# Who transposes K, in which units, and in what order x and q0 are formed: six edits to the first third of a sliding-window attention kernel

## The chip, the cores and the metric

The kernel runs on one core of one Trainium2 chip. The metric is the device time of one execution in microseconds (us); lower is better. A time quoted for a kernel is the median of its runs, usually four: one with a profile and three timed rounds. Positions inside a kernel are microseconds from the start of the span of its one profiled execution, which is some 2 us shorter than the device time. Ratios are always against the kernel before in the same rounds on the same chip (medians 185.15 to 186.0 us), so compare kernels of different rounds by their ratios.

The engines are PE (matmuls and transposes through PE), PEld (PE's weight loads), DVE (vector), ACT (the exponentials), POOL (here used for small moves), and SP, which issues nearly all DMAs. PSUM is the memory that PE writes to in this kernel and that DVE and ACT copy out of.

## The reference

Eight sequences of 32 queries attend to the last 2,048 keys of a cache. There are 32 query heads and 4 K/V heads, so that 8 query heads share one K. Everything is bf16; the head size is 128.

```python
B, Sq, D = 8, 32, 1024
Hq, Hkv, Sk, Dh = 32, 4, 8192, 128
W = min(4096, max(256, Sk // 4))                  # 2048
q = transpose((x @ wq).reshape(B, Sq, Hq, Dh))
k = repeat(k_cache[:, :, Sk - W:, :], 8 heads); v = the same of v_cache
p = softmax((q @ k^T) * Dh ** -0.5)
out = transpose(p @ v).reshape(B, Sq, Hq * Dh) @ wo
```

## The kernel before

The work is cut into 32 units, one for each pair of K/V head and sequence. A unit's K is 2,048 x 128 and has 256 query columns. A unit has four slots, so that unit u is slots 4u to 4u+3. A slot is 4 score matmuls (`s_ps`), one exponential on ACT, and the 8 `o_ps` matmuls of the slot two earlier. Into slots PE also takes pieces of other work: transposes of a later K, the projections q1 to q3 of the later heads, and the output projection. I write S(n) for the start of slot n's score matmuls.

The score matmul needs K transposed. Three routes do it, chosen by unit:

- `PE_T`: K arrives as it is, PE transposes it in 16 pieces into PSUM, DVE copies it out.
- `V_T`: K arrives as it is, DVE turns its 32 x 32 blocks in four instructions (`kb`), then POOL puts the blocks in place in up to 16 moves (`kTv`).
- otherwise: two transposing DMAs, each of half of K (256 KB).

```python
Q_CUT = 6
N_WARM = (8, 0, 0)
PE_T = (0, 1, 2, 3, 4)
# unit: (load with unit, slots of the 4 DVE block transposes, first and end slot of the moves, moves on POOL of 16)
V_T = {5: (2, (5, 6, 8, 10), 10, 17, 12),
       **{u: (u - 4, range(4*u - 16, 4*u - 12), 4*u - 13, 4*u - 4, 16) for u in (8, 11, 14, 17, 20, 23, 26, 29)}}
Q_SLOTS = {1: (17, 31), 2: (38, 54), 3: (69, 83)}       # slots in which q1, q2, q3 are formed

def kv_pieces(self, ui):
    def blocks(i):                                         # DVE
        ...
        nc.vector.transpose(out=st["kb"][:, sl, :], in_=self.k_raw[ui][:, sl, :])
    def move(k, d):                                        # POOL, or DVE beyond the unit's share
        ...
        if d >= V_T[ui][4] // 4:
            nc.vector.tensor_copy(out=out, in_=in_)
        else:
            nc.gpsimd.tensor_scalar(out=out, in0=in_, scalar1=1.0, scalar2=1.0, op0=ALU.mult, op1=ALU.mult)
...
# the start: x in two tiles of 128 rows, on two queues
nc.sync.dma_start(out=x_sb[:, 0, :], in_=xf[0:P, :])
nc.scalar.dma_start(out=x_sb[:, 1, :], in_=xf[P:2 * P, :])
wq0 = self.load_wq(0, 0, (1, 1, 1, 1)) + self.load_wq(0, 1, (2, 1, 1))    # q0's weights, in 7 pieces
...
def x_turn(half, pl, tag):                 # both row tiles of one half of the columns
    ps = pl.tile([P, H, self.NT, P], BF16, name="xT_ps", tag=tag)
    for c in range(H):
        for t in range(self.NT):
            nc.tensor.transpose(ps[:, c, t, :], x_sb[:, t, half*H + c:self.D:self.DC], self.ident[:, :])
    for i, copy in ((0, nc.vector.tensor_copy), (1, nc.scalar.copy)):
        ...
x_turn(0, self.ps_m, "m")
x_turn(1, self.ps_s, "s_ps")
...
for c in range(self.DC):                   # q0: 8 heads; from c = 6 on only the first 128 rows
    for h in range(self.rep):
        q_mm(c, h, 0, P if c >= Q_CUT else self.NQ)
    ...
...                                        # the cut rest of q0 is done in slots 0 and 1
```

`N_WARM` counts the matmuls of no use that PE does before x has come.

POOL takes the moves in program order, and so does DVE its block transposes and copies; there are two buffers each for `kb` and `kTv`.

Of the kernel before, what the change touches and what calls it, by code (L numbers as in the profile page):

```python
# [18 lines left out]
Q_CUT = 6  # L19
N_WARM = (8, 0, 0)  # L20
# [3 lines left out]
PE_T = (0, 1, 2, 3, 4)  # L24

V_T = {5: (2, (5, 6, 8, 10), 10, 17, 12),
       **{u: (u - 4, range(4 * u - 16, 4 * u - 12), 4 * u - 13, 4 * u - 4, 16) for u in (8, 11, 14, 17, 20, 23, 26, 29)}}
W_AT = (3, 3, 4, 4, 8, 8, 9, 9, 11, 12, 13, 13, 14, 15, 16, 16, 18, 19, 19, 20, 22, 22, 23, 24, 25, 26, 28, 28)

Q_SLOTS = {1: (17, 31), 2: (38, 54), 3: (69, 83)}  # L30
# [74 lines left out]
class Fast:  # L105
# [101 lines left out]
    def load_unit(self, ui):  # L207

        if ui < len(self.units):
            if ui not in V_T:  # L210
                self.load_k(ui, None if ui in PE_T else 0)
            self.load_v(ui, self.nc.sync)
            if ui not in V_T and ui not in PE_T:
                self.load_k(ui, 1)
        for u, at in V_T.items():
            if at[0] == ui:
                self.load_k(u)
        for p, at in zip(self.weights, W_AT):
            if at == ui:
                p()  # L220
# [46 lines left out]
    def q_pieces(self, g):  # L267
        nc, P, DC = self.nc, self.P, self.DC
        st = {}

        def piece(hl, i):
            if i == 0:
                st["ps"] = self.ps_m.tile([P, 512], FP32, name="q_ps", tag="m")
            for c in range(i * DC // 2, (i + 1) * DC // 2):
                nc.tensor.matmul(st["ps"][:, 0:self.NQ], lhsT=self.wq_t[g, i][:, c % (DC // 2), hl * P:(hl + 1) * P],  # L275
                                 rhs=self.xT[:, c, :], start=(c == 0), stop=(c == DC - 1))
            if i == 1:
                nc.vector.tensor_copy(out=self.q_view(g)[:, :, hl, :],  # L278
                                      in_=st["ps"][:, 0:self.NQ].rearrange("p (b s) -> p b s", b=self.B))
        return [lambda h=h, i=i: piece(h, i) for h in range(self.rep) for i in range(2)]  # L280
# [31 lines left out]
    def start(self):  # L312
# [8 lines left out]
        nc.scalar.dma_start(out=x_sb[:, 1, :], in_=xf[P:2 * P, :])  # L321
# [25 lines left out]
        warm_up(N_WARM[0])  # L347


        def x_turn(half, pl, tag):  # L350
            ps = pl.tile([P, H, self.NT, P], BF16, name="xT_ps", tag=tag)
            for c in range(H):
                for t in range(self.NT):
                    nc.tensor.transpose(ps[:, c, t, :], x_sb[:, t, half * H + c:self.D:self.DC], self.ident[:, :])  # L354
            for i, copy in ((0, nc.vector.tensor_copy), (1, nc.scalar.copy)):
                c0 = half * H + i * H // 2
                copy(out=self.xT[:, c0:c0 + H // 2, :], in_=ps[:, i * H // 2:(i + 1) * H // 2, :, :].rearrange("p c t s -> p c (t s)"))

        x_turn(0, self.ps_m, "m")
        x_turn(1, self.ps_s, "s_ps")  # L360
        qs = [pl.tile([P, 2, self.NQ], FP32, name="q0_ps", tag=tag)
              for pl, tag in ((self.ps_o, "o_ps"), (self.ps_o, "o_ps"), (self.ps_m, "m"), (self.ps_m, "m"))]
# [11 lines left out]
        def q_mm(c, h, n0, n1):  # L374
            nc.tensor.matmul(qs[h // 2][:, h % 2, n0:n1], lhsT=self.wq_t[0, c // H][:, c % H, h * P:(h + 1) * P],  # L375
                             rhs=self.xT[:, c, n0:n1], start=(c == 0 and h % 2 == 0), stop=(c == self.DC - 1),
                             skip_group_check=True)

        for c in range(self.DC):
            for h in range(self.rep):  # L380
                q_mm(c, h, 0, P if c >= Q_CUT else self.NQ)
            if c == 0:
                warm_up(N_WARM[2])
                warm_sb = self.c1.tile([P, 8], BF16, name="warm_sb")
                nc.vector.tensor_copy(out=warm_sb[:, :], in_=warm[:, 0:8])
            if c == self.DC - 3:
                tp = self.ps_s.tile([P, KT, P], BF16, name="kf_ps", tag="s_ps")
                k_turn(0)
                k_copy(0)
        k_turn(1)  # L390

        def q_copy(eng, k, b0, b1):
            src = qs[k][:, :, :].rearrange("p h (b s) -> p b h s", b=self.B)[:, b0:b1, :, :]
            dst = self.q_view(0)[:, b0:b1, k * 2:(k + 1) * 2, :]
            (nc.vector.tensor_copy if eng == "v" else nc.scalar.copy)(out=dst, in_=src)
        for k, eng in ((0, "a"), (1, "v"), (2, "a"), (3, "v")):
            q_copy(eng, k, 0, 1)
        k_copy(1)
        self.va_copy(0)

        def q_rest(k):
            for h in (2 * k, 2 * k + 1):
                for c in range(Q_CUT, self.DC):
                    q_mm(c, h, P, self.NQ)
            q_copy("v", k, 1, self.B)
        self.q_rest = [lambda k=k: q_rest(k) for k in (0, 2, 3, 1)]
# [19 lines left out]
    def side_plan(self):  # L426
# [4 lines left out]
        def spread(pieces, s0, s1):  # L431
            for k, p in enumerate(pieces):
                plan[s0 + (s1 - s0) * k // len(pieces)].append(p)
        for g, w in Q_SLOTS.items():
# [10 lines left out]
    def run(self):  # L445
# [3 lines left out]
        for i, p in enumerate(self.q_rest):  # L449
            plan[i // 2].append(p)  # L450
# [205 lines left out]
```

## Time and profile before

The kernel took 185.55 us as given (185.06 to 186.25).

| what | before |
|---|---|
| span of the profile | 183.3 us |
| PE busy | 178.7 us, 98% |
| POOL busy | 94.7 us, 52% |
| first score matmul, S(0) | 12.92 us |
| S(31), S(32), S(48) | 51.12, 52.01, 70.73 us |
| last score matmuls, S(127) | 172.23 us |

The first fence has lines of the profile page: busy time of each engine with its share of the span and its instruction count; the shares of the chain that ended last, by engine; and two groups of instructions (line, engine, operation, output<-input, shapes, count | busy us, mean ns | idle us ahead of them and what ended most of it); and the transposing DMAs (count, median us from issue to landing).

```profile
PE 178.7 (98%) x2041; PEld 153.6 (84%) x2057; DVE 114.8 (63%) x266; ACT 131.6 (72%) x133; POOL 94.7 (52%) x150
...
PE 96%; DMA 2%; issue 1%; DVE 0%
...
L261 POOL TENSOR_SCALAR kTv<-kb 32x512 bf16<-32x512 bf16 x140 | 93.7, 670 | 63.8 <-PE s_ps L467 37.3
...
L236 PE MATMUL tp<-ident,k_raw 128*128 128x128 bf16 x64 | 5.9, 219 | 0.0
...
kT<-in_k_cache_dram SPq DMA_TRANSPOSE x36, 6.5
```

PE is the limit, and the chain says that it is so nearly everywhere. POOL looks half idle. The timeline of POOL shows what that average hides. Its columns are start in us, length in us, engine, line, operation, count, and in brackets the idle time before and what ended it.

```profile
27.03 8.77 POOL L261 TENSOR_SCALAR kTv<-kb 32x512 bf16<-32x512 bf16 x12 [25.46 <-PE s_ps L467]
38.44 11.77 POOL L261 TENSOR_SCALAR kTv<-kb 32x512 bf16<-32x512 bf16 x16 [2.64 <-PE s_ps L467]
53.18 11.65 POOL L261 TENSOR_SCALAR kTv<-kb 32x512 bf16<-32x512 bf16 x16 [2.97 <-DVE kb L251]
66.85 11.65 POOL L261 TENSOR_SCALAR kTv<-kb 32x512 bf16<-32x512 bf16 x16 [2.02 <-DVE kb L251]
```

These are the K of units 5, 8, 11 and 14, or K5, K8, K11 and K14 for short. The 16 moves of a K last 11.65 to 11.77 us, and POOL has two to three idle microseconds between them. K8 is ready at 50.21 and needed at 52.01; K11 is ready at 64.83 and needed at 65.42. So POOL just keeps up, with turned units that lie three apart.

The last fence is the timeline of PE, same columns: the start, then the score matmuls that open units 8, 9 and 12 (slots 32, 36 and 48).

```profile
4.50 1.33 PE L354 MATMUL xT_ps<-ident,x_sb 128*128 128x128 bf16 x16
5.84 5.40 PE L375 MATMUL q_ps<-xT,wq_sb 128*128 128x256 bf16 x48
12.92 0.60 PE L467 MATMUL s_ps<-QT,kT 128*128 128x256 bf16 x4
...
52.01 0.60 PE L467 MATMUL s_ps<-QT,kTv 128*128 128x256 bf16 x4
55.63 0.60 PE L467 MATMUL s_ps<-QT,kT 128*128 128x256 bf16 x4
70.73 0.60 PE L467 MATMUL s_ps<-QT,kT 128*128 128x256 bf16 x4
```

No line of PE carries a bracket: PE waits for nobody in all this stretch. Anything that makes it wait is paid in full.

### The profile page before, as it was taken

Reading aid. Unit: us, or ns where it says so; the run is one execution under the profiler, and the core shown is the slowest. Engines: PE = TensorE matmul, PEld = TensorE weight load, DVE = VectorE, ACT = ScalarE, POOL = GpSimd, SP = SyncE. Lnnn points to the kernel's source line nnn. Section 1 sums busy time; section 2 is a strip of 40 time slices with the busy share of each in tenths; the row PEclk is TensorE's granted clock in tenths of the full one; section 3 lists DMA queues with packets and bytes.
Section 4 is the critical chain, followed back from the end, with each engine's and each line's share of the span. In section 5 each row is a group of like instructions: output and inputs, shape, how many; then the busy total and the mean of one; then the engine's idle time right before and its main releaser. Section 6 shows DMA issues by size and latency. Waiting matters only on the chain.

```text
span 183.3 us, 5041 instructions
## 1 busy us (share of the span) xinstructions
PE 178.7 (98%) x2041; PEld 153.6 (84%) x2057; DVE 114.8 (63%) x266; ACT 131.6 (72%) x133; POOL 94.7 (52%) x150
## 2 busy tenths in 40 slices
PE   7999999999999999999999999999999999999993
PEld 2899999999999999987878999987787888888843
DVE  0238899975584774685567558647755865365363
ACT  2218999777799877777786687787877888888800
POOL 2000019759839959929945980896299279600000
DMA  6999999999999999999999999989999999960003
GB/s 173 392 405 407 397 402 367 186 249 397 258 307 303 384 240 325 401 246 249 378 380 227 374 389 224 245 327 386 242 371 345 216 272 286 229 185 1 0 32 93
DMA packets 52954, 51.73 MB, mean 282 GB/s; under 512 B 39744, under 2 KB 40256, under 8 KB 52928
## 3 DMA queue, kind: packets, MB, share of 16 engines
q1 hardware_dynamic: 52352, 50.90, 98.3%
q10 hardware_dynamic: 576, 0.49, 0.8%
q8 instruction: 16, 0.26, 0.6%
q14 instruction: 10, 0.08, 0.1%
HBM read 41.42 MB, written 0.52 MB: 229 GB/s over the span
## 4 chain that ended last, share of the span: by engine, by line
PE 96%; DMA 2%; issue 1%; DVE 0%
PE o_ps L478 32%; PE s_ps L467 31%; PE op_ps L295 14%; PE q_ps L275 11%; PE q_ps L375 4%; DMA x_sb<-in_x_dram 2%; PE tp L236 2%; PE xT_ps L354 1%; PE kf_ps L368 1%; DVE o_t L305 0%; PE cnt_ps L532 0%
## 5 line engine op out<-in xcount | busy, mean ns | idle before, releaser
L469 ACT ACTIVATE pT<-s_ps 128x1024 bf16<-128x1024 f32 x128 | 128.8, 1025 | 32.4 <-PE s_ps L467 31.4
L261 POOL TENSOR_SCALAR kTv<-kb 32x512 bf16<-32x512 bf16 x140 | 93.7, 670 | 63.8 <-PE s_ps L467 37.3
L478 PE MATMUL o_ps<-va,pT 128*128 128x129 bf16 x1024 | 78.8, 220 | 0.1
L478 PEld LDWEIGHTS <-pT 128*128 128x128 bf16 x1024 | 68.5, 98 | 3.1
L467 PE MATMUL s_ps<-QT,kT 128*128 128x256 bf16 x368 | 55.2, 273 | 0.2
L467 PEld LDWEIGHTS <-kT 128*128 128x128 bf16 x368 | 34.8, 98 | 10.3
L295 PE MATMUL op_ps<-wo_sb,OT 128*128 128x512 bf16 (+2 forms) x128 | 32.7, 352 | 0.6
L275 PE MATMUL q_ps<-xT,wq_sb 128*128 128x256 bf16 x192 | 28.1, 273 | 0.0
L409 DVE COPY va<-v_sb 128x2048 bf16<-128x2048 bf16 x32 | 25.3, 789 | 0.1
L251 DVE STREAM_TRANSPOSE kb<-k_raw 128x512 bf16<-128x512 bf16 x36 | 23.8, 685 | 0.0
L415 DVE RECIPROCAL RL_all<-o_ps 128x2 f32<-128x2 f32 x32 | 5.2, 164 | 27.5 <-PE o_ps L478 27.5
L467 PE MATMUL s_ps<-QT,kTv 128*128 128x256 bf16 x144 | 21.6, 272 | 0.0
L420 DVE TENSOR_SCALAR o_sb<-o_ps,RL_all 128x128 bf16<-128x128 f32 x64 | 19.5, 346 | 1.1
L467 PEld LDWEIGHTS <-kTv 128*128 128x128 bf16 x144 | 13.9, 98 | 5.1
L278 DVE CAST QT<-q_ps 128x256 bf16<-128x256 f32 x24 | 9.8, 406 | 13.4 <-PE q_ps L275 13.4
L275 PEld LDWEIGHTS <-wq_sb 128*128 128x128 bf16 x192 | 17.0, 98 | 1.2
L422 DVE STREAM_TRANSPOSE OT<-o_sb 128x256 bf16<-128x256 bf16 x32 | 14.3, 445 | 1.1
L295 PEld LDWEIGHTS <-OT 128*128 128x128 bf16 x144 | 11.4, 98 | 2.3 <-DVE OT L422 0.2
L302 DVE TENSOR_TENSOR oacc<-op_ps,oacc 128x512 f32<-128x512 f32 x8 | 5.5, 682 | 7.4 <-PE op_ps L295 7.4
L375 PE MATMUL q_ps<-xT,wq_sb 128*128 128x256 bf16 (+1 forms) x80 | 7.7, 251 | 0.0
L375 PEld LDWEIGHTS <-wq_sb 128*128 128x128 bf16 x80 | 6.7, 98 | 0.7
L236 PE MATMUL tp<-ident,k_raw 128*128 128x128 bf16 x64 | 5.9, 219 | 0.0
(30 smaller groups left out, 36.6 us busy)
## 6 DMA issues: line engine op xcount, KB each, us to landing
v_sb<-in_v_cache_dram SPq DMA_DIRECT2D x30, 512.0 KB, 7.0
wo_sb<-in_wo_dram SPq DMA_DIRECT2D x16, 512.0 KB, 6.5
wq_sb<-in_wq_dram SPq DMA_DIRECT2D x13, 512.0 KB, 7.3
k_raw<-in_k_cache_dram SPq DMA_DIRECT2D x13, 512.0 KB, 5.9
wq_sb<-in_wq_dram SPq DMA_DIRECT2D x6, 256.0 KB, 4.6
v_sb<-in_v_cache_dram SPq DMA_DIRECT2D x4, 256.0 KB, 4.8
kT<-in_k_cache_dram SPq DMA_TRANSPOSE x36, 6.5
k_raw<-in_k_cache_dram SPq DMA_DIRECT2D x2, 256.0 KB, 5.8
```

The lines of the kernel that those rows point to most:

```text
L251: nc.vector.transpose(out=st["kb"][:, sl, :], in_=self.k_raw[ui][:, sl, :])
L261: nc.gpsimd.tensor_scalar(out=out, in0=in_, scalar1=1.0, scalar2=1.0, op0=ALU.mult, op1=ALU.mult)
L275: nc.tensor.matmul(st["ps"][:, 0:self.NQ], lhsT=self.wq_t[g, i][:, c % (DC // 2), hl * P:(hl + 1) * P], rhs=self.xT[:, c, :], start=(c == ...
L278: nc.vector.tensor_copy(out=self.q_view(g)[:, :, hl, :], in_=st["ps"][:, 0:self.NQ].rearrange("p (b s) -> p b s", b=self.B))
L295: nc.tensor.matmul(ps[:, 0:w], lhsT=self.OT[:, gq, c, t * P:(t + 1) * P], rhs=self.wo_t[gq][:, c, n0:n0 + w], start=(k == 0), stop=(k == 7))
L375: nc.tensor.matmul(qs[h // 2][:, h % 2, n0:n1], lhsT=self.wq_t[0, c // H][:, c % H, h * P:(h + 1) * P], rhs=self.xT[:, c, n0:n1], start=(c ...
L409: self.nc.vector.tensor_copy(out=self.va[ui % 3][:, :, 0:self.Dh], in_=self.v_sb[ui][:, :, :])
L420: nc.vector.tensor_scalar(out=o_sb[:, qt, :, :], in0=o_ps[:, qt, 0:Dh].rearrange("p (i c) -> p c i", c=4), scalar1=rl[:, ui * QT_N + qt:ui ...
L422: nc.vector.transpose(out=self.OT[:, g * QT_N:(g + 1) * QT_N, :, b * self.Sq:(b + 1) * self.Sq], in_=o_sb[:, :, :, :])
L467: nc.tensor.matmul(s_ps[:, jj, :], lhsT=self.kT[ui][:, c * CJ + jj, :], rhs=q_u, start=True, stop=True)
L469: nc.scalar.activation(out=pT[:, :, :], in_=s_ps[:, :, :], func=ACT.Exp, bias=0.0, scale=self.scale)
L478: nc.tensor.matmul(o_ps[:, qt, 0:self.VW], lhsT=pT[:, jj, qt * P:(qt + 1) * P], rhs=va[:, j, 0:self.VW], start=(j == 0 and qt == 0), stop= ...
```

## The change

Six edits, meant to relieve PE or to let it start earlier:

1. K3 and K4 go from PE to transposing DMAs. That is 32 PE transposes less.
2. In exchange for DMA room, the V route turns units 8, 10, 12, 15, 17 and so on (not 8, 11, 14, 17): one K more, and closer together. Block transposes and moves are issued one slot later, those of unit 8 three slots later (the last block transpose in slot 22, not 19).
3. q0: the second row half of heads 4 to 7 leaves the start and is done in slots 0, 1, 8 and 10 (`q_late`).
4. q1 is formed from slot 14 on (in unit 3), not from slot 17, and its pieces are ordered so that the second half of its weights is needed later.
5. x is transposed by row tiles, the first tile without waiting for the second, and both tiles are loaded by SP's queue.
6. Where weights and the raw K of a V unit are loaded at the same unit, the weights now go first.

```diff
-Q_CUT = 6
-N_WARM = (8, 0, 0)
+N_WARM = 7
-PE_T = (0, 1, 2, 3, 4)
+PE_T = (0, 1, 2)
 V_T = {5: (2, (5, 6, 8, 10), 10, 17, 12),
-       **{u: (u - 4, range(4 * u - 16, 4 * u - 12), 4 * u - 13, 4 * u - 4, 16) for u in (8, 11, 14, 17, 20, 23, 26, 29)}}
+       8: (4, range(19, 23), 22, 30, 16),
+       **{u: (u - 4, range(4 * u - 15, 4 * u - 11), 4 * u - 12, 4 * u - 4, 16) for u in (10, 12, 15, 17, 20, 23, 26, 29)}}
-Q_SLOTS = {1: (17, 31), 2: (38, 54), 3: (69, 83)}
+Q_LATE = {0: (0, 2), 1: (8, 12)}
+Q_SLOTS = {1: (14, 31), 2: (38, 54), 3: (69, 83)}
 ... load_unit: the pieces of the weights ahead of the raw K of the V units
 ... q_pieces: two heads share a PSUM tile; for q1 four heads' first weight half comes before their second
+    def q_late(self, h0): ...      # rows 128 to 255 of two heads of q0, one PSUM tile, one DVE copy
-        nc.scalar.dma_start(out=x_sb[:, 1, :], in_=xf[P:2 * P, :])
+        nc.sync.dma_start(out=x_sb[:, 1, :], in_=xf[P:2 * P, :])
-        def x_turn(half, pl, tag): ...
+        def x_turn(t):
+            ps = self.ps_s.tile([P, 2, self.DC, P], BF16, name="xT_ps", tag="s_ps")
             for i, copy in ((0, nc.vector.tensor_copy), (1, nc.scalar.copy)):
+                for c in range(H):
+                    nc.tensor.transpose(ps[:, i, c, :], x_sb[:, t, i * H + c:self.D:self.DC], self.ident[:, :])
+                copy(out=self.xT[:, i * H:(i + 1) * H, t * P:(t + 1) * P], in_=ps[:, i, 0:H, :])
 ... the copies of q0 by row halves
```

More of the change, by code (lines that the diff above doesn't have):

```diff
@@ L214, in load_unit @@
                 self.load_k(ui, 1)
+        for p, at in zip(self.weights, W_AT):
+            if at == ui:
+                p()
         for u, at in V_T.items():
@@ L217, in load_unit @@
                 self.load_k(u)
-        for p, at in zip(self.weights, W_AT):
-            if at == ui:
-                p()
     def k_pieces(self, ui):
@@ L271, in piece @@
         def piece(hl, i):
+            k = hl // 2
+            if i == 0 and hl % 2 == 0:
+                st[k] = self.ps_m.tile([P, 2, self.NQ], FP32, name="q_ps", tag="m")
+            for c in range(i * DC // 2, (i + 1) * DC // 2):
+                nc.tensor.matmul(st[k][:, hl % 2, :], lhsT=self.wq_t[g, i][:, c % (DC // 2), hl * P:(hl + 1) * P],
+                                 rhs=self.xT[:, c, :], start=(c == 0 and hl % 2 == 0), stop=(c == DC - 1), skip_group_check=True)
+            if i == 1 and hl % 2 == 1:
+                nc.vector.tensor_copy(out=self.q_view(g)[:, :, 2 * k:2 * k + 2, :].rearrange("p b h s -> p h b s"),
+                                      in_=st[k][:, :, :].rearrange("p h (b s) -> p h b s", b=self.B))
@@ L272, in piece, with q_late @@
+        n = 4 if g == 1 else 2
+        return [lambda h=h, i=i: piece(h, i) for h0 in range(0, self.rep, n) for i in range(2) for h in range(h0, h0 + n)]
+    def q_late(self, h0):
+        nc, P, DC, B = self.nc, self.P, self.DC, self.B
+        st = {}
+        def piece(i):
             if i == 0:
-                st["ps"] = self.ps_m.tile([P, 512], FP32, name="q_ps", tag="m")
-            for c in range(i * DC // 2, (i + 1) * DC // 2):
-                nc.tensor.matmul(st["ps"][:, 0:self.NQ], lhsT=self.wq_t[g, i][:, c % (DC // 2), hl * P:(hl + 1) * P],
-                                 rhs=self.xT[:, c, :], start=(c == 0), stop=(c == DC - 1))
+                st["ps"] = self.ps_m.tile([P, 2, P], FP32, name="ql_ps", tag="m")
+            for c in range(DC):
+                nc.tensor.matmul(st["ps"][:, i, :], lhsT=self.wq_t[0, c // (DC // 2)][:, c % (DC // 2), (h0 + i) * P:(h0 + i + 1) * P],
+                                 rhs=self.xT[:, c, P:self.NQ], start=(c == 0 and i == 0), stop=(c == DC - 1), skip_group_check=True)
@@ L277, in piece @@
             if i == 1:
-                nc.vector.tensor_copy(out=self.q_view(g)[:, :, hl, :],
-                                      in_=st["ps"][:, 0:self.NQ].rearrange("p (b s) -> p b s", b=self.B))
-        return [lambda h=h, i=i: piece(h, i) for h in range(self.rep) for i in range(2)]
+                nc.vector.tensor_copy(out=self.q_view(0)[:, B // 2:, h0:h0 + 2, :].rearrange("p b h s -> p h b s"),
+                                      in_=st["ps"][:, :, :].rearrange("p h (b s) -> p h b s", b=B // 2))
@@ L282, in o_pieces @@
+        return [lambda i=i: piece(i) for i in range(2)]
     def o_pieces(self, g, t, cuts=(512, 512), st=None):
@@ L346, in warm_up @@
                 nc.tensor.matmul(warm[:, :], lhsT=one(1.0, [P, P], BF16), rhs=one(1.0, [P, 512], BF16), start=True, stop=True)
-        warm_up(N_WARM[0])
-        def x_turn(half, pl, tag):
-            ps = pl.tile([P, H, self.NT, P], BF16, name="xT_ps", tag=tag)
-            for c in range(H):
-                for t in range(self.NT):
-                    nc.tensor.transpose(ps[:, c, t, :], x_sb[:, t, half * H + c:self.D:self.DC], self.ident[:, :])
-            for i, copy in ((0, nc.vector.tensor_copy), (1, nc.scalar.copy)):
-                c0 = half * H + i * H // 2
-                copy(out=self.xT[:, c0:c0 + H // 2, :], in_=ps[:, i * H // 2:(i + 1) * H // 2, :, :].rearrange("p c t s -> p c (t s)"))
-        x_turn(0, self.ps_m, "m")
-        x_turn(1, self.ps_s, "s_ps")
-        qs = [pl.tile([P, 2, self.NQ], FP32, name="q0_ps", tag=tag)
-              for pl, tag in ((self.ps_o, "o_ps"), (self.ps_o, "o_ps"), (self.ps_m, "m"), (self.ps_m, "m"))]
+        warm_up(N_WARM)
+        warm_sb = self.c1.tile([P, 8], BF16, name="warm_sb")
+        nc.vector.tensor_copy(out=warm_sb[:, :], in_=warm[:, 0:8])
+        def x_turn(t):
+            ps = self.ps_s.tile([P, 2, self.DC, P], BF16, name="xT_ps", tag="s_ps")
+            for i, copy in ((0, nc.vector.tensor_copy), (1, nc.scalar.copy)):
+                for c in range(H):
+                    nc.tensor.transpose(ps[:, i, c, :], x_sb[:, t, i * H + c:self.D:self.DC], self.ident[:, :])
+                copy(out=self.xT[:, i * H:(i + 1) * H, t * P:(t + 1) * P], in_=ps[:, i, 0:H, :])
+        x_turn(0)
+        x_turn(1)
+        qs = [self.ps_o.tile([P, 2, self.NQ], FP32, name="q0_ps", tag="o_ps") for _ in range(2)]
+        qs.append(self.ps_m.tile([P, 4, P], FP32, name="q0_ps", tag="m"))
         KT = self.KT
@@ L372, in k_copy, with q_mm, q_copy @@
             nc.vector.tensor_copy(out=self.kT[0][:, sl, :], in_=tp[:, sl, :])
-        def q_mm(c, h, n0, n1):
-            nc.tensor.matmul(qs[h // 2][:, h % 2, n0:n1], lhsT=self.wq_t[0, c // H][:, c % H, h * P:(h + 1) * P],
-                             rhs=self.xT[:, c, n0:n1], start=(c == 0 and h % 2 == 0), stop=(c == self.DC - 1),
+        def q_mm(c, h):
+            ps, n = (qs[h // 2][:, h % 2, :], self.NQ) if h < 4 else (qs[2][:, h - 4, :], P)
+            nc.tensor.matmul(ps, lhsT=self.wq_t[0, c // H][:, c % H, h * P:(h + 1) * P],
+                             rhs=self.xT[:, c, 0:n], start=(c == 0 and h in (0, 2, 4)), stop=(c == self.DC - 1),
                              skip_group_check=True)
+        def q_copy(copy, h0, h1, b0, b1):
+            ps = qs[h0 // 2] if h0 < 4 else qs[2]
+            copy(out=self.q_view(0)[:, b0:b1, h0:h1, :].rearrange("p b h s -> p h b s"),
+                 in_=ps[:, :, b0 * self.Sq:b1 * self.Sq].rearrange("p h (b s) -> p h b s", s=self.Sq))
         for c in range(self.DC):
-            for h in range(self.rep):
-                q_mm(c, h, 0, P if c >= Q_CUT else self.NQ)
-            if c == 0:
-                warm_up(N_WARM[2])
-                warm_sb = self.c1.tile([P, 8], BF16, name="warm_sb")
-                nc.vector.tensor_copy(out=warm_sb[:, :], in_=warm[:, 0:8])
-            if c == self.DC - 3:
+            if c == self.DC - 2:
                 tp = self.ps_s.tile([P, KT, P], BF16, name="kf_ps", tag="s_ps")
@@ L389, in start @@
                 k_copy(0)
+            for h in range(self.rep):
+                q_mm(c, h)
         k_turn(1)
-        def q_copy(eng, k, b0, b1):
-            src = qs[k][:, :, :].rearrange("p h (b s) -> p b h s", b=self.B)[:, b0:b1, :, :]
-            dst = self.q_view(0)[:, b0:b1, k * 2:(k + 1) * 2, :]
-            (nc.vector.tensor_copy if eng == "v" else nc.scalar.copy)(out=dst, in_=src)
-        for k, eng in ((0, "a"), (1, "v"), (2, "a"), (3, "v")):
-            q_copy(eng, k, 0, 1)
+        q_copy(nc.scalar.copy, 0, 2, 0, 1)
+        q_copy(nc.vector.tensor_copy, 2, 4, 0, 1)
+        q_copy(nc.scalar.copy, 4, 8, 0, 1)
         k_copy(1)
         self.va_copy(0)
-        def q_rest(k):
-            for h in (2 * k, 2 * k + 1):
-                for c in range(Q_CUT, self.DC):
-                    q_mm(c, h, P, self.NQ)
-            q_copy("v", k, 1, self.B)
-        self.q_rest = [lambda k=k: q_rest(k) for k in (0, 2, 3, 1)]
+        q_copy(nc.vector.tensor_copy, 0, 2, 1, self.B)
+        q_copy(nc.vector.tensor_copy, 2, 4, 1, self.B)
+        q_copy(nc.vector.tensor_copy, 4, 8, 1, self.B // 2)
     def va_copy(self, ui):
@@ L433, in spread @@
                 plan[s0 + (s1 - s0) * k // len(pieces)].append(p)
+        for k, w in Q_LATE.items():
+            spread(self.q_late(4 + 2 * k), *w)
         for g, w in Q_SLOTS.items():
@@ L448, in run @@
         plan = self.side_plan()
-        for i, p in enumerate(self.q_rest):
-            plan[i // 2].append(p)
         pv_queue = []
```

## The prediction

> **What bounds it now.** PE. The page has PE busy 98% of 183.3 us; the chain of waits is 96% PE, and between 4.5 us (x lands) and about 172 us PE never waits. In the timeline a slot (4 score matmuls + 8 o_ps matmuls) takes 0.89 us bare, 1.11 with 4 K transposes, 1.33 with 4 q matmuls. ACT (1025 ns an exponential) is hidden except in bare slots (0.92). POOL looks idle half the time (52%), but by unit it is tight: the 16 moves of one V-turned K take 11.65 us on the timeline (12 moves of K5: 8.77), and end 0.3 us (K5), 1.8 (K8), 0.6 (K11), 0.7 (K29) before PE's first score of that unit.
>
> **What goes, costed from the trace.**
> - 32 PE transposes of K3, K4: 0.22 us per 4, so -1.8 us of PE.
> - x: tile 0's transposes no longer wait for tile 1; first q0 matmul about 0.4 us earlier.
> - q0: the same columns (4 heads x 128 rows moved out of the start), PE total unchanged; the start loses 0.9 us that returns in slots 0 to 10. But wq's third piece landed at 8.65 us, so about 0.5 us of the earlier start is spent waiting. First score at about 12.4 us (12.92 before).
> - Without new waits: -1.4 us, everywhere.
>
> **What it adds.**
> - DMA: K3 and K4 become transposing DMAs in the backlogged first 35 us. There a plain 512 KB landing costs 1.28 us (about 410 GB/s); a transposed half of K (256 KB) about 1.0 to 1.2. The Trainium skill, DMA: Bandwidth & Descriptors, Latency and other measured facts, gives 261 GB/s for a transposing DMA; the trace agrees roughly (210 to 260). K4's second half should land at 30 to 31.5 us, against a need at about 30.2; q1's second weight half at 33 to 34, against 33.8. I expect 0 to 2 us of PE waits here, 0.7 likely.
> - POOL, the large one. V now turns 8, 10, 12, 15 instead of 8, 11, 14. Spaced three units apart, 12 slots of 1.33 (16 us) covered 11.65. Two apart, 8 slots give 7 to 10.6 us. POOL cannot start K8 before its fourth block transpose, now issued in slot 22 (before: 19) behind q1's copy: about 2 us after slot 22's scores. Then K8, K10, K12 are 48 moves back to back, 35 us (the first four of K10 even stand before K8's last two). PE's own work from slot 22 to slot 48 (unit 12) is about 31 us. So PE must lose about 6 us, in three waits: before unit 8 about 2 to 2.5, before unit 10 about 2, before unit 12 about 1 to 1.5. Slot 48 starts near 76 us (70.7 before).
> - Later V units start one slot later than before; slack shrinks, K29 may cost 0.3 us.
> - DVE: about neutral (4 copies of 0.65 less, 4 block transposes of 0.69 more).
>
> **On the critical path:** PE's saving counts fully, but only until slot 22; POOL's queue then decides. From unit 12 on PE is dense again, as before, so nothing is won back.
>
> **Predicted:** 191.2 us, range 189.0 to 193.0. Faster 0.01, same 0.17, slower 0.82.
>
> **Signs.** Right: PE idle before s_ps of kTv tiles of units 8, 10, 12, about 6 us released by POOL kTv; POOL unbroken from about 40 to 76 us; kTv moves 156 at about 670 ns; transposes of K 32 on that line instead of 64; DMA-transposes 38. Slot 32 to 48 longer than 20 us.
>
> **Wrong if** POOL's moves run faster with less DVE traffic; if DMA waits for K3 or K4 are far larger (then slot 22 slips, more than 193); if slot 22's block transpose comes earlier than I place it (then 189).

## The result, and the profile after

The changed kernel took 193.75 us (192.66 to 194.5) against 185.31 us: slower by a ratio of 1.0445, 95% interval 1.0374 to 1.0515. A ratio is the mean time of one kernel's runs over that of the other's of the same rounds, so it is not quite the ratio of the medians quoted. The direction was as predicted, the size was not: 193.75 lies 0.75 us above the range of 189.0 to 193.0.

Lines of the changed kernel's page. The new one, PEclk, is the clock granted to PE in 40 equal slices of the span, in tenths; the kernel before has no such line.

```profile
PE 180.8 (94%) x2024; PEld 154.4 (81%) x2040; DVE 112.8 (59%) x254; ACT 131.6 (69%) x133; POOL 103.6 (54%) x166
...
PEclk9999999999996999999999999999999999999998
...
PE 81%; POOL 12%; DVE 2%; issue 2%; ACT 1%; ACTq 0%
...
L262 POOL TENSOR_SCALAR kTv<-kb 32x512 bf16<-32x512 bf16 x156 | 102.7, 658 | 63.3 <-DVE kb L252 38.5
...
kT<-in_k_cache_dram SPq DMA_TRANSPOSE x38, 7.1
```

POOL has come into the chain with 12%, and PE's share of the span fell to 94%. Next, the waits of PE in the changed kernel (who waited, for what: total us, how often, the longest).

```profile
PE s_ps L479 <- POOL kTv L262: 4.4, 3, 3.8
PE xT_ps L374 <- DVE xT L375: 1.0, 2, 0.5
```

POOL's timeline after. The 48 moves of K8, K10 and K12 are now a single line: unbroken from 43.61 to 77.97 us.

```profile
28.57 8.71 POOL L262 TENSOR_SCALAR kTv<-kb 32x512 bf16<-32x512 bf16 x12 [27.00 <-DVE kb L252]
43.61 34.36 POOL L262 TENSOR_SCALAR kTv<-kb 32x512 bf16<-32x512 bf16 x48 [6.34 <-issue]
```

PE's timeline after: the start, then the end of slot 31 and the opening of slots 32, 33, 36, 40 and 48.

```profile
3.72 0.63 PE L374 MATMUL xT_ps<-ident,x_sb 128*128 128x128 bf16 x4
4.87 1.01 PE L374 MATMUL xT_ps<-ident,x_sb 128*128 128x128 bf16 x8 [0.52 <-DVE xT L375]
6.39 0.59 PE L374 MATMUL xT_ps<-ident,x_sb 128*128 128x128 bf16 x4 [0.51 <-DVE xT L375]
6.78 5.46 PE L394 MATMUL q_ps<-xT,wq_sb 128*128 128x256 bf16 x48
14.36 0.60 PE L479 MATMUL s_ps<-QT,kT 128*128 128x256 bf16 x4
...
52.40 0.62 PE L490 MATMUL o_ps<-va,pT 128*128 128x129 bf16 x8
56.77 0.61 PE L479 MATMUL s_ps<-QT,kTv 128*128 128x256 bf16 x4 [3.75 <-POOL kTv L262]
57.98 1.06 PE L479 MATMUL s_ps<-QT,kTv 128*128 128x256 bf16 x4
61.99 0.60 PE L479 MATMUL s_ps<-QT,kT 128*128 128x256 bf16 x4
66.91 0.61 PE L479 MATMUL s_ps<-QT,kTv 128*128 128x256 bf16 x4 [0.31 <-POOL kTv L262]
78.03 0.61 PE L479 MATMUL s_ps<-QT,kTv 128*128 128x256 bf16 x4 [0.34 <-POOL kTv L262]
```

Two things stand out. The start has two holes, its transposes are slow, and the first score comes 1.44 us later than before rather than earlier. And PE stands for 3.75 us before unit 8; the next slot's four score matmuls then take 1.06 us in place of 0.60, since the trace's clock record has PE at half clock from 57.31 to 60.72 us.

With the slot starts of both timelines, the 8.2 us by which the span grew divide as follows. The right column is the prediction's own sum.

| stretch | before | changed | difference | predicted |
|---|---|---|---|---|
| to S(0) | 12.92 | 14.36 | +1.44 | -0.5 |
| S(0) to S(31) | 38.20 | 37.60 | -0.60 | -0.2 (0.9 less PE work, 0.7 DMA waits) |
| S(31) to S(48) | 19.61 | 26.07 | +6.46 | +6 |
| S(48) to S(127) | 101.50 | 101.94 | +0.44 | +0.3 |
| after S(127) | 11.1 | 11.5 | +0.5 | 0 |
| sum | | | +8.2 | +5.6 |

So the largest term was nearly right, and of the 2.6 us that are missing in the sum the start has 1.9. This start was an unusual one, though. Four other traces with the same start (V units apart, the same filled, half of the moves on DVE, the changed kernel once more) have the first score at 13.49 to 13.61; five traces with the start of the kernel before have it at 12.85 to 13.34. The two groups do not overlap, and their means differ by 0.65 us. With the changed kernel's second trace the start has 1.1 of 1.9 us missing.

### The profile page after: what moved, and what is told of

The parts are those of the page before. It is cut to its first block, busy times and chain, and to the rows that moved or that the text cites. A ratio compares the mean times of both kernels' runs of the same rounds, so it can differ in the third digit from the quotient of the medians.

```text
span 191.5 us, 5015 instructions
## 1 busy us (share of the span) xinstructions
PE 180.8 (94%) x2024; PEld 154.4 (81%) x2040; DVE 112.8 (59%) x254; ACT 131.6 (69%) x133; POOL 103.6 (54%) x166
## 4 chain that ended last, share of the span: by engine, by line
PE 81%; POOL 12%; DVE 2%; issue 2%; ACT 1%; ACTq 0%
PE o_ps L490 26%; PE s_ps L479 25%; PE op_ps L313 14%; POOL kTv L262 12%; PE q_ps L277 9%; PE q_ps L394 3%; PE warm_ps L364 2%; PE xT_ps L374 1%; PE tp L237 1%; DVE QT L400 1%; ACT pT L481 1%; PE kf_ps L386 0%; PE ql_ps L293 0%; DVE xT L375 0%; DVE kT L390 0%
## 5 line engine op out<-in xcount | busy, mean ns | idle before, releaser
L262 POOL TENSOR_SCALAR kTv<-kb 32x512 bf16<-32x512 bf16 x156 | 102.7, 658 | 63.3 <-DVE kb L252 38.5
L490 PE MATMUL o_ps<-va,pT 128*128 128x129 bf16 x1024 | 79.7, 221 | 0.1
L479 PE MATMUL s_ps<-QT,kT 128*128 128x256 bf16 x352 | 52.8, 273 | 0.1
L479 PEld LDWEIGHTS <-kT 128*128 128x128 bf16 x352 | 33.3, 98 | 10.2
L479 PE MATMUL s_ps<-QT,kTv 128*128 128x256 bf16 x160 | 25.0, 280 | 4.7 <-POOL kTv L262 4.4
L252 DVE STREAM_TRANSPOSE kb<-k_raw 128x512 bf16<-128x512 bf16 x40 | 26.3, 684 | 0.0
L479 PEld LDWEIGHTS <-kTv 128*128 128x128 bf16 x160 | 15.6, 101 | 11.1 <-POOL kTv L262 5.9
L277 PEld LDWEIGHTS <-wq_sb 128*128 128x128 bf16 x192 | 16.9, 98 | 1.1
L280 DVE CAST QT<-q_ps 128x512 bf16<-128x512 f32 x12 | 8.0, 668 | 6.6 <-PE q_ps L277 6.6
L394 PEld LDWEIGHTS <-wq_sb 128*128 128x128 bf16 x64 | 5.9, 112 | 0.8
L390 DVE COPY kT<-kf_ps 128x1024 bf16<-128x1024 bf16 x2 | 1.4, 692 | 6.8 <-PE kf_ps L386 6.8
```

The costliest lines, as they stand in the source:

```text
L277: nc.tensor.matmul(st[k][:, hl % 2, :], lhsT=self.wq_t[g, i][:, c % (DC // 2), hl * P:(hl + 1) * P], rhs=self.xT[:, c, :], start=(c == 0 a ...
L280: nc.vector.tensor_copy(out=self.q_view(g)[:, :, 2 * k:2 * k + 2, :].rearrange("p b h s -> p h b s"), in_=st[k][:, :, :].rearrange("p h (b ...
L394: nc.tensor.matmul(ps, lhsT=self.wq_t[0, c // H][:, c % H, h * P:(h + 1) * P], rhs=self.xT[:, c, 0:n], start=(c == 0 and h in (0, 2, 4)), ...
L479: nc.tensor.matmul(s_ps[:, jj, :], lhsT=self.kT[ui][:, c * CJ + jj, :], rhs=q_u, start=True, stop=True)
L490: nc.tensor.matmul(o_ps[:, qt, 0:self.VW], lhsT=pT[:, jj, qt * P:(qt + 1) * P], rhs=va[:, j, 0:self.VW], start=(j == 0 and qt == 0), stop= ...
```

## The experiments

Theory: POOL's queue of 48 moves sets slot 48, whatever PE does between; the remaining miss lies in the start. Rivals: DMA contention of the new transposes causes the loss; POOL is slow for other reasons than spacing; or the start does not count, since POOL's queue decides slot 48 anyway.

### Undo the x edit alone

```diff
-N_WARM = 7
+N_WARM = 8
-        nc.sync.dma_start(out=x_sb[:, 1, :], in_=xf[P:2 * P, :])
+        nc.scalar.dma_start(out=x_sb[:, 1, :], in_=xf[P:2 * P, :])
 ... x_turn of the kernel before, by column halves
```

> The changed kernel with the loading and turning of x as before (second row tile on the ACT queue, all 16 transposes of x without a wait between, 8 warm-up matmuls); all else as changed. Theory (two costs that add: a slow start, then POOL's queue): first score near 12.5 to 12.9 us instead of 14.4, the q0 matmuls 109 and 56 ns apart from the first one, POOL starts K8 about 1.5 us earlier because slot 22 comes earlier, the three PE waits before units 8, 10, 12 stay at about 4.5 us or more in sum; time about 192.1 us (1.4 to 1.8 less than the changed kernel). Rival (POOL's queue alone, held by DMA landings and not by PE's slots): POOL starts K8 at the same time, time unchanged at 193.7.

Measured: 193.14 us, ratio 1.0379 (1.0318 to 1.0441). PE's timeline of this kernel has no holes in the start:

```profile
5.88 4.30 PE L396 MATMUL q_ps<-xT,wq_sb 128*128 128x256 bf16 x48
...
12.30 0.60 PE L481 MATMUL s_ps<-QT,kT 128*128 128x256 bf16 x4
```

The first score now comes at 12.30, where the prediction had put it (12.4). Slot 22 came at 39.03 (40.45), POOL began K8 at 42.19 (43.61), and slot 48 came at 76.69 (78.03). POOL's start moved with slot 22, so the rival that the start does not count falls. The ratio is 0.66 of a per cent lower than the changed kernel's, about 1.2 us; the intervals overlap, so the evidence is the 1.3 us by which slot 48 moved in the trace rather than the times. Part of that is chance: against the second trace of the changed kernel (below, slot 48 at 77.40) it is 0.7 us.

### V units three apart again, the rest as changed

```diff
-    ... 4 * u - 12, 4 * u - 4, 16) for u in (10, 12, 15, 17, 20, 23, 26, 29)}}
+    ... 4 * u - 12, 4 * u - 4, 16) for u in (11, 14, 17, 20, 23, 26, 29)}}
```

> The changed kernel, but V turns K of 8, 11, 14, 17, ... (three apart), units 10, 12, 15 by DMA. Theory (POOL's queue): only a wait before unit 8 is left (about 2.4 us: 16 moves from 43.6 us against slot 32 at 52.9), none before 11 and 14; slot 48 near 74 instead of 78; time about 189.7 us. Rival (the added transposing DMAs of the early stretch are what costs): no gain, 193 or more, and PE waits for DMA.

Measured: 190.47 us, ratio 1.0237. The waits before units 10 and 12 are gone, and none came before 11 or 14. One wait stays, before unit 8, whose schedule is the same as in the changed kernel. PE's timeline:

```profile
54.87 0.87 PE L479 MATMUL s_ps<-QT,kTv 128*128 128x256 bf16 x4 [2.61 <-POOL kTv L262]
56.40 1.06 PE L479 MATMUL s_ps<-QT,kTv 128*128 128x256 bf16 x4
60.09 0.60 PE L479 MATMUL s_ps<-QT,kT 128*128 128x256 bf16 x4
```

From slot 32 to 36 it takes 5.22 us, where the kernel before takes 3.62. The clock record has half clock from 55.09 to 58.50. So this wait costs 2.6 us and then 1.6 us more, and the second part was not in my expectation (189.7). The rival of DMA contention falls: PE waits for a DMA only once, 0.5 us for q0's weights.

### The same with PE kept busy through the wait

Ten matmuls of no use into a spare PSUM tile, ahead of slot 32.

```diff
+                if ui == 8 and c == 0:
+                    fill = self.ps_m.tile([P, 512], FP32, name="fill_ps", tag="m")
+                    for _ in range(10):
+                        nc.tensor.matmul(fill[:, :], lhsT=<constant 1.0>, rhs=<constant 1.0>, start=True, stop=True)
```

> The kernel of the run with V three apart, and ten dummy matmuls of 512 columns on constants (about 2.2 us) before unit 8's first scores, inside PE's wait of 2.8 us there. Theory (a wait of that length also costs the clock: after it PE ran one stretch of 3.4 us at half clock, about 1.6 us lost): no half-clock stretch near 55 us, slots 32 to 36 take 3.6 us instead of 5.2; time about 188.9 us (190.5 without). Rival (the clock drop has nothing to do with the wait): unchanged or longer, 190.5 or more.

Measured: 189.36 us, ratio 1.0207 (1.0169 to 1.0245). PE's timeline:

```profile
52.04 2.35 PE L480 MATMUL fill_ps<-const-bfloat16-1.0 128*128 128x512 bf16 x10
54.81 0.61 PE L484 MATMUL s_ps<-QT,kTv 128*128 128x256 bf16 x4 [0.42 <-POOL kTv L262]
58.42 0.60 PE L484 MATMUL s_ps<-QT,kT 128*128 128x256 bf16 x4
```

Slot 32 starts at the same time (54.81 to 54.87), and slot 36 is 1.67 us earlier, for the clock stays full. The half clock is gone in the timed rounds too: the mean granted clock for each run is 0.989 to 0.991 without the filling and 0.999 to 1.0 in the three timed rounds with it. The gain in time is only 0.3% (0.6 us) by the ratios, less than the intervals can settle. One source of that noise can be seen: in the profiled execution slot 127 came 1.89 us earlier than without the filling (175.23 against 177.12), yet the span is 188.7 against 188.5, because the last pieces of the output landed 3.6 to 3.8 us after their issue and not 1.5 to 2.0. In all fourteen traces the engines' work from slot 127 on takes 8.6 us; two of them (this one and the run with K4 alone) have such a late landing, of about 2 us, and it has nothing to do with the edits of the first third.

### Give POOL half of the moves, DVE the other half

```diff
-       8: (4, range(19, 23), 22, 30, 16),
+       8: (4, range(19, 23), 22, 30, 8),
-    ... 4 * u - 4, 16) for u in (10, 12, ...)
+    ... 4 * u - 4, 8 if u < 15 else 16) for u in (10, 12, ...)
```

> The changed kernel, units 8, 10, 12 still turned two apart, but half of their moves (8 of 16) done by DVE instead of POOL. Theory: POOL needs about 5.8 us for each of the three and is done before PE asks; the waits before 8, 10, 12 fall below 0.5 us in sum; slot 48 near 71.6; time about 187.3 us; what stays over the kernel before is the start (1.7 us) less the transposes. Rival (DVE has no room, it is the DVE that is late): DVE's delay moves the wait to another line and the time stays above 190.

Measured: 191.94 us, ratio 1.0328. My expectation of 187.3 missed. PE's waits:

```profile
PE o_ps L490 <- DVE va L421: 2.5, 3, 1.3
PE s_ps L479 <- DVE kTv L260: 2.2, 1, 2.2
```

POOL was done with a K's eight moves in 5.3 to 5.7 us, and PE waited for DVE in its place. A move takes 0.28 to 0.66 us on DVE (0.46 in the median), and DVE also copies V (`va`) for the coming unit; it is 66% busy over the whole of this run, but it has no room at the moment it matters. The rival that DVE would become the limit was right.

### The closer V spacing alone, in the kernel before

```diff
-    ... for u in (8, 11, 14, 17, 20, 23, 26, 29)}}
+    ... for u in (8, 10, 12, 15, 17, 20, 23, 26, 29)}}
```

> The kernel before with one part of the change alone: V turns 8, 10, 12, 15 instead of 8, 11, 14. Theory: POOL starts K8 at 38.4 us as before, 48 moves of 0.72 us end at about 73 us, unit 12 begins at 73.2 instead of 70.7; time about 188.0 us, all of the difference as PE waits for POOL. Rival (the spacing only hurts together with the later loads of the change): 185.3, no waits.

Measured: 187.9 us, ratio 1.0089 (1.003 to 1.0148). The time is as expected; the loss, 1.9 us against the 186.0 of these rounds, is a little less than the 2.7 expected. POOL's timeline:

```profile
38.87 34.76 POOL L261 TENSOR_SCALAR kTv<-kb 32x512 bf16<-32x512 bf16 x48 [2.63 <-PE s_ps L467]
```

PE's waits:

```profile
PE s_ps L467 <- POOL kTv L261: 2.2, 2, 1.8
```

The same unbroken 48 moves put slot 48 at 73.69, 3.0 us later than before (70.73), where the changed kernel has it 7.3 us later (78.03). The difference is POOL's start: 38.87 here, 43.61 in the changed kernel, where the last block transpose of K8 is issued in slot 22, not 19. From POOL's start to slot 48 both take nearly the same, 34.8 and 34.4 us. Of the 3.0 us, 0.4 is chance: this execution had its first score at 13.34 and everything up to POOL's start as much later. So of the 7.3 us the spacing has about 2.5, and POOL's start, 5.2 us later than before (43.61 against 38.44), has the rest: 1.7 because slot 22 came later (40.45 against 38.74), and about 3 by the later issue of K8. That last part is worked out by subtraction; no run has the later issue alone. No transposing DMAs were added here: POOL loses this without them.

### K3 and K4 by DMA alone, in the kernel before

```diff
-PE_T = (0, 1, 2, 3, 4)
+PE_T = (0, 1, 2)
```

> The kernel before with one part alone: K of units 3 and 4 by transposing DMA, PE transposes units 0 to 2 only; V as before. Theory: 1.8 us of PE work gone, but the queue is slower by some 2 us up to q1's second weight half, which this kernel needs already at slot 18: PE waits 2 to 4 us for wq there, and unit 5's moves (0.3 us of slack before) come late by about 1 us where the wait does not cover it; time 185.5 to 188. Rival (transposing DMAs are free here): 183.9, PE without waits.

Measured: 189.94 us, ratio 1.0226. PE's waits, and the clock line of the page in the second fence:

```profile
PE q_ps L275 <- DMA wq_sb<-in_wq_dram: 4.2, 2, 2.4
```

```profile
PEclk9999999659999999999999999999999999999999
```

The weights of q1 come too late, and half clock from 34.9 to 41.7 us follows. The two runs with a granted clock of 0.98 took 191.1 us, the two with 0.991 took 188.5 and 188.8. The mechanism was expected, the size was not (185.5 to 188). So in the kernel before this edit needs the order of q1 of edit 4, which the next run adds. In the changed kernel, which has it and edit 6, PE's waits have no DMA line at all.

### K3 and K4 by DMA with the order of q1 mended

```diff
-PE_T = (0, 1, 2, 3, 4)
+PE_T = (0, 1, 2)
-V_T = {5: (2, (5, 6, 8, 10), 10, 17, 12),
+V_T = {5: (2, (5, 6, 8, 10), 10, 17, 8),
+       8: (4, range(18, 22), 21, 30, 16),
 ... the other units as before; q_pieces of the change
```

> The run with K3 and K4 by DMA in the kernel before, now with q1's order of the change, half of unit 5's moves on DVE and unit 8's block transposes two slots later (its K lands later). Theory (that run lost its time at q1's second weight half, needed at slot 18): the 4 us of waits for the weights and the half-clock stretch after them vanish; a wait of 0 to 1.5 us before unit 8; time 184 to 186, ratio 0.993 to 1.003. Rival (the transposing DMAs starve PE anywhere in this stretch): still 188 or more.

Measured: 186.64 us, ratio 1.0044 (1.0007 to 1.0081). PE's timeline at unit 8:

```profile
52.92 0.61 PE L470 MATMUL s_ps<-QT,kTv 128*128 128x256 bf16 x4 [1.24 <-POOL kTv L262]
```

The loss of the run above is gone, without edit 6: PE waits for no weights, and slot 31 came at 50.63, half a microsecond earlier than before. POOL takes it back at unit 8, with a wait of 1.24 us. Earlier work of PE is worth nothing when POOL's K8 is what it arrives at. (The ratio lies just above the 0.993 to 1.003 expected.)

### K4 alone

```diff
-PE_T = (0, 1, 2, 3, 4)
+PE_T = (0, 1, 2, 3)
-V_T = {5: (2, (5, 6, 8, 10), 10, 17, 12),
+V_T = {5: (2, (5, 6, 8, 10), 10, 17, 8),
 ... q_pieces of the change
```

> A smaller step from the kernel before: K of unit 4 alone by transposing DMA, q1's pieces in the change's order (four heads' first halves, then their second halves), half of unit 5's moves on DVE; V units as before. Theory: 16 PE transposes less (0.89 us), the queue about 1 us later, which the new order of q1 absorbs; no PE wait over 0.3 us; about 184.5 us, ratio 0.995. If POOL's slack (0.3 us at unit 5) or the loads are still too tight, no gain.

Measured, with five rounds: 187.06 us, ratio 1.0057 (1.002 to 1.0094). I had expected 184.5, a small gain. In its trace PE waits 0.9 us for DVE's copy of V and 0.3 us for its copy of q1, and slot 32 came at 52.56 (52.01). DVE had been given four more moves of K5, which is the likely cause of its lateness, but no run parts it from the other edits. Sixteen transposes less on PE did not pay for that. The size is less sure than the ratio looks: the six runs fall into two groups, 186.19 to 186.52 and 187.6 to 187.88, and the profiled one (187.88) has the late landing of the output described above. Even the faster group lies above the kernel before (185.56).

### V units shifted by one, three apart, with x as before

```diff
-    8: (...), ... for u in (10, 12, 15, 17, 20, 23, 26, 29)
+    **{u: (u - 4, range(4*u - 16, 4*u - 12), 4*u - 13, 4*u - 4, 16) for u in (9, 12, 15, 18, 21, 24, 27, 30)}
-Q_SLOTS = {1: (14, 31), ...
+Q_SLOTS = {1: (16, 31), ...
 ... x_turn, N_WARM and x's queue of the kernel before
```

> An attempt at a version that beats both: the changed kernel with x as before, q1 from slot 16, and V turning 5, 9, 12, 15, ... 30 (three apart, shifted by one, each with its blocks one slot earlier). Theory: first score near 12.4, no PE wait over 0.5 us before any unit, slot 32 near 51.0 (before 52.0); time about 1.0 us under the kernel before (ratio 0.994). If POOL's start for unit 9 slips, a wait of 1 to 2 us there and the ratio is 1.00 to 1.01.

Measured: 190.59 us (188.69 to 191.5), ratio 1.0303. It should have beaten the kernel before (0.994). Until slot 32 it did: 51.26, without a wait for POOL. The waits of PE, then those of DVE:

```profile
PE o_ps L491 <- DVE va L422: 3.6, 3, 2.6
```

```profile
DVE kb L251 <- DMA k_raw<-in_k_cache_dram: 16.2, 7, 4.2
```

DVE's block transposes now stand before raw K that has not landed (K12 landed at 55.54). DVE takes its work in program order here (V's copy ran at 59.23, after the last of them), so V's copy behind them waits too, and PE with it. In the traced execution the limit has moved to DMA; it was the fastest of the four runs, and why the others took 1.2 to 2.8 us more is not shown. Of the versions that I tried none beats the kernel before.

### Where the start loses: transposes in one go

```diff
 def x_turn(t):
-            for i, copy in ((0, nc.vector.tensor_copy), (1, nc.scalar.copy)):
+            for i in range(2):
                 for c in range(H):
                     nc.tensor.transpose(...)
+            for i, copy in ((0, nc.vector.tensor_copy), (1, nc.scalar.copy)):
                 copy(...)
```

> The changed kernel, x still by row tiles on one queue, but all 8 transposes of a row tile are issued before its two copies (before: 4, copy, 4, copy, so PE waited for the copy each time). Theory (the start lost its time to that hand-over between PE and DVE, and to the half clock that the holes prolong): PE goes through x without a hole of 0.8 us, first q0 matmul at 5.6 to 5.9 us instead of 6.8, first score near 12.3; time about 192.4 us, as with x undone. Rival (the second row tile on the same queue pushes the weights of q0 back, 5.86 instead of 5.20 us, and q0 waits for them): first score still near 13.3 or later, time unchanged.

Measured: 193.3 us, ratio 1.0434. The gain did not come: the first q0 matmul at 6.35, the first score at 14.38. In this execution the clock rose only at 10.08 us, and the fifth of the seven pieces of q0's weights landed at 10.70. Taking out the holes alone is not enough.

### The changed kernel once more

No edit.

> The changed kernel once more, unaltered, for a second trace of its start. Theory (of the start's loss about 1.2 us is the way x is turned and its weights land later, the rest depends on where the clock's 3.4 us windows happen to fall): first score at 13.5 us if the clock rises before 6.2 us, at 14.4 if it rises near 9.5 to 10; either way later than 12.3 to 12.6; time 192.6 to 194.5. Rival (the late clock always belongs to the change): 14.4 and a clock that rises near 9.5 again.

Measured: 192.96 us, ratio 1.0401 (1.0357 to 1.0445). In this trace the clock rose at 3.79 us, and the start looks otherwise. PE's timeline:

```profile
9.92 1.49 PE L394 MATMUL q_ps<-xT,wq_sb 128*128 128x256 bf16 x16 [1.03 <-DMA wq_sb<-in_wq_dram]
...
13.54 0.60 PE L479 MATMUL s_ps<-QT,kT 128*128 128x256 bf16 x4
```

With the clock in its favour the first score is 0.82 us earlier than in the first trace, and still 0.62 us later than in the kernel before. What is left over is a DMA: the fifth piece of q0's weights (the prediction calls it the third) landed at 9.88 us, against 8.65 before. Both tiles of x go ahead of the weights on the same queue, so the first piece is issued at 1.66 us instead of 1.20. In the six traces with this queue the fifth piece landed at 9.20 to 10.70, in the eight with x's second tile on ACT's queue at 8.64 to 9.28. A DMA that was hidden behind a slow clock in one trace is the limit in the other.

### Grouped transposes with x's second tile on ACT's queue

```diff
-N_WARM = 7
+N_WARM = 8
-        nc.sync.dma_start(out=x_sb[:, 1, :], in_=xf[P:2 * P, :])
+        nc.scalar.dma_start(out=x_sb[:, 1, :], in_=xf[P:2 * P, :])
 ... and the grouped transposes of the run before last
```

> The changed kernel with x still turned by row tiles, transposes grouped ahead of the copies, but the second row tile loaded on the ACT queue as before and 8 warm-ups. Theory (what the grouped run still lost was the later landing of the weights, issued one place later on the SP queue, and a PE that begins x in the cold clock): first weights land at 5.2 to 5.3 us instead of 5.6 to 5.9, first q0 matmul at 5.8 to 6.0, first score 12.3 to 12.6; time 1.2 us less than the changed kernel on the same chip. Rival (turning by row tiles itself is what costs): first score 13.3 or later.

Measured: 192.05 us, ratio 1.0354, against the 192.96 of the unedited kernel on the same chip. PE's timeline:

```profile
6.38 4.12 PE L395 MATMUL q_ps<-xT,wq_sb 128*128 128x256 bf16 x48 [0.52 <-DVE xT L376]
...
12.62 0.60 PE L480 MATMUL s_ps<-QT,kT 128*128 128x256 bf16 x4
```

Here q0 starts later than in the unedited kernel (6.38 against 6.09) and ends sooner, because the weights are there: the first piece landed at 4.84 us, the fifth at 8.73. The first score comes at 12.62 and slot 48 at 76.60 (77.40 unedited). So x by row tiles is not itself the fault. With the clock up early, the queue is; the holes then lie ahead of a wait that would be there anyway. (This rests on the traces. The intervals of the two ratios overlap, and grouping without the new queue was traced only with a late clock.)

## Why the prediction was wrong, and what of it was right

**What bounds the kernel: right.** PE without waits before; each wait that the change created is found in the time.

**POOL's queue: right in mechanism, sum and sign.** All the signs came: 38 transposing DMAs and 32 transposes of K on PE, moves 156 (mean 658 ns), unbroken from 43.61 to 77.97, PE released by `kTv` before units 8, 10 and 12, and slot 32 to 48 taking 21.3 us. The sum of 6.46 us against "about 6" is fair. Its division was off. Before unit 8 PE stood 3.75 us, not 2 to 2.5, since POOL began 3.2 us after slot 22 and not 2: DVE had the cast of slot 21 (at 41.61) and two block transposes (42.18 to 43.46) ahead of it. Before 10 and 12 it stood 0.3 us each, not 2 and 1 to 1.5, for two reasons: the first wait had taken more of the sum, and PE at half clock spent 1.6 us working slowly (slots 32 to 36 took 5.22 us, not 3.62). The parts are 3.75 + 0.31 + 0.34 + 1.6 = 6.0 us. That half clock was not in the prediction, but it cost nothing extra here, for POOL's queue set slots 40 and 48. In the version with the V units apart it did cost, 1.6 us in its trace.

**DMA: the size was too large.** The prediction had 0.7 us of waits. K4's second half landed at 31.68 and q1's second weight half at 34.41, both a little later than estimated, and PE waited for neither. A transposed half landed 0.82 to 0.91 us after the transfer before it, better than the 1.0 to 1.2 estimated; the trace of the kernel before already had 0.81 to 0.89 for halves that landed right behind another transfer. Run alone in the kernel before, the edit cost 4 us of waits; with q1's order of the change no wait for weights was left. So that order earns what the term had feared. What edit 6 adds to it no run shows.

**PE's saving: right in size, worth nothing.** From the first score to slot 31 the changed kernel is 0.6 us faster. As the prediction said, POOL then decides.

**K29 and the rest:** 0.43 us at K29 against 0.3. About 0.5 us after the last score matmuls was in no term. The traces place it: the engines' work from slot 127 on takes 8.62 us in both, and the end of the span comes 1.43 us after the last piece of output has landed, against 0.89 before. Its cause is not shown.

**The step that failed** reads: "First score at about 12.4 us (12.92 before)." It came at 14.36 in the profile, and at 13.54 in the second one. That is +1.4 and +0.6 where -0.5 was predicted. The step behind it, a first q0 matmul "about 0.4 us earlier", failed too: it came at 6.78 and 6.09, against 5.84 before. The prediction saw that a first tile no longer waits for the second. It did not see two things that the same edit does. It puts both tiles of x ahead of the q0 weights on one queue, so their fifth piece lands 1.2 us later (9.88 against 8.65, in the second profile). It makes PE wait twice, 0.5 us each, for DVE to copy the first half of a PSUM tile out. In the first trace a third thing came on top: PE at half clock during q0, until 9.52 us. The Trainium skill, "TensorE: Matmul & The Clock Gate", Part 1: The HAM clock gate, says that the clock's window is free-running and that the point of transition therefore varies; the traces agree that it varies, and by far more than the 500 ns that the page gives: in the five traces with the changed kernel's start the rise came at 3.79, 3.89, 5.77, 5.88 and 9.52 us, and over all versions at 3.48 to 10.08. So the late clock of the first trace is nothing that the edit brings each time; four of the five rose early. That the holes cause a late rise was argued and is not shown: the version with its transposes in one go had the latest of all.

As the start moves slot 22, and slot 22 moves POOL, the miss went through to the end: slot 48 at 78.03 in place of 76, and 76.69 and 76.60 in the two versions whose start is as assumed. The time of the first of those, by its ratio to the kernel before, is 1.0379 x 185.31 = 192.3 us (191.2 to 193.5 by its interval). That lies within the range, and above its middle by the small terms named.

**The range was too narrow.** Its upper end lay 1.8 us above the estimate. A second measurement of the same kernel gave 192.96, just inside. The start alone differs by 0.8 us from one execution to the other, which one profile of the kernel before could not show.

## What to carry to other kernels

An engine that is half idle over the span can be the limit of a stretch; cost a denser schedule by that engine's longest unbroken queue and by what releases its first item, for all that PE saves ahead of it is then given back. When a reordering lets one load or transpose begin sooner, follow the whole queue behind it, and ask where PE will now stand still: a hand-over that was hidden behind a wait becomes a hole. A wait of two to four microseconds may also cost a stretch at half clock (here 3.4 or 6.8 us long), so fill it, or make it shorter; it costs time only where nothing else sets the next stretch.

## What the Trainium skill lacked or had wrong

- "TensorE: Matmul & The Clock Gate", Part 1: The HAM clock gate. It gives a window of 3413 ns, and half clock "after ≥1 idle window (~3.4µs)". The traces agree on the length: half clock lasted 3.413 us in the changed kernel, and 6.83 us, two windows, in its second profile. They differ on the trigger, which need not be a whole idle window: a PE wait of 2.61 us sufficed in one run, while waits of 1.8 and 2.6 us in two others were not followed by half clock. The traces tell why. Counted from the first rise of the clock, every later change up to the last score lies a whole number of windows on (57.31 is 14 windows after 9.52). What counts is how long PE stood idle within one such window. In seven traces a window had 1.99 to 3.08 us of it, and half clock followed at its end; no window at full clock with 1.82 us or less was followed by half clock. The 2.6 us wait without consequence was cut by a window's edge into 1.04 and 1.60. The full clock came back after one window when PE's idle time in it was at most 0.69 us (four traces), after two when it was 0.98 us or more (three). That section gives no such share.
- The same section gives 106.7 ns a matmul cold and 55.6 warm for 128 columns. In the changed kernel the x transposes are 107 ns apart at half clock and the eight of K0, at full clock, 56 ns (0.45 us from the first to the matmul after them). This agrees.
- "DMA: Bandwidth & Descriptors", Latency and other measured facts. It gives 261 GB/s for a transposing DMA with a non-contiguous middle dimension and about 350 to 400 for a contiguous one. Here a half of K (256 KB, read in runs of 2 KB out of every 4 KB) took 0.82 to 0.91 us behind another transfer, which works out at 290 to 320 GB/s: between the two. The page does not say which of its figures holds for such a source.
- "GPSIMD Engine Reference", 3.1 Elementwise, gives 1.03 cycles an element for the body of a simple operation and, for 512 elements in a tight loop, 769 ns measured. A 32x512 bf16 move by POOL took 658 to 670 ns busy and 0.716 us from one to the next in a series of 48 (34.36 / 48). That is between 439 ns (512 x 1.03 / 1.2 GHz, an estimate with the page's clock) and 769; the section has no figure for such a move from partitions to other partitions.
